# A gated recurrence followed by an MLP on one core: a list scheduler in the kernel sets every engine's order, the activation becomes a linear term plus relu(-h)

## The chip, the cores and the metric

The kernel runs on one core of one Trainium2 chip. The metric is device time in microseconds (us): 1410.16 us before, the median of three runs between 1408.06 and 1410.41. The core's engines are TensorE (PE, matmuls; PEld, its weight loads), VectorE (DVE), ScalarE (ACT) and GpSimd (POOL). SyncE (SP) issues DMA transfers. Each engine works through its own instructions strictly in the order in which the program holds them, and semaphores tie the engines together. So an instruction that waits also holds up all that stands behind it on its engine.

## The reference

Batch 4, 8 heads, sequence 768, head dimension 48, all float32. A complex gate decays a state matrix per head; then an MLP works on the 3072 tokens.

```python
def _attn_ref(q, k, v, a_re, a_im):
    mag = np.sqrt(a_re * a_re + a_im * a_im)
    scale = np.minimum(mag, 0.999) / (mag + 1e-06)
    a_re_n, a_im_n = (a_re * scale, a_im * scale)
    for t in range(S):
        ar, ai = (a_re_n[:, :, t, :, None], a_im_n[:, :, t, :, None])
        new_re = ar * S_re - ai * S_im
        new_im = ar * S_im + ai * S_re
        kv = np.einsum('bhd,bhe->bhde', k[:, :, t], v[:, :, t])
        S_re, S_im = (new_re + kv, new_im)
        y[:, :, t] = np.einsum('bhd,bhde->bhe', q[:, :, t], S_re)
def _moe_ref(x, w_in, w_out, alpha):     # x: 3072 x 384, d_ff 2048
    h = x @ w_in
    g = np.maximum(h, 0.0) + alpha * np.minimum(h, 0.0)
    return g @ w_out
```

## The kernel before

The recurrence is worked in 24 units, one for each batch and each chunk of 128 tokens (`NU = 24`, `NCH = 6` chunks a batch).

- `gates` turns a_re and a_im into decays (`decs`) and rotations (`phs`) for one to three chunks at once. It is a long chain between DVE and ACT: the normalised gate, then running complex products in groups of eight (`product`, three DVE instructions each), then a scan over the groups. Both results go to DRAM.
- `first_halves` copies half rows of v, for five of the level widths, from DRAM to DRAM (`vsc`, L330); `load` brings a unit's q, k, rotations `PP`, decays `T`, and v in several layouts into SBUF. It loads q and k twice (L342/L343 and again L349/L350). All DMAs are issued from SP.
- `unit` multiplies q and k by the rotation (L369), then goes through levels of width 1, 2, 4 ... 64. For each level `meet` makes scores on PE (`ps_lv`, L378), masks them on DVE or ACT (L388, L386, L382), and DVE multiplies halves of q and k by decays (L427). Level 1 has an extra product of the odd rows ("odd"). Then the state is updated (`ps_kt`, `ps_kv`, `St`) and the outputs are summed (`ps_y`, L465, L472), copied to `yT` and written to DRAM as `ysc` (L482).
- `weights` converts w_in and w_out from 64-bit words in 32 pieces (`to_f32`: two ACT, four DVE and two POOL instructions a piece, L297 and L298), in the three `ot` buffers.
- `mlp` takes two units (256 tokens): 16 times three matmuls of w_in with `xT` (L495), relu(-h) on ACT (L499), h + (1 - alpha) relu(-h) on DVE (L501), then 2 x 16 matmuls with w_out (L508).

What sets the order: a loop over slots (`LAG = 6` slots a unit). In each slot the live units go one step on; `gates`, `weights`, `first_halves` and `mlp` are spread over given stretches of slots by `spread`. A fp32 matmul of the program shows as two records in the trace, so that 576 matmuls of L495 are x1152 there; a transpose is one record.

Of the kernel before, what the change touches and what calls it, by code (L numbers as in the profile page):

```python
# [15 lines left out]
P = 128  # L16
# [5 lines left out]
F64_SMALL = 2.0 ** -15 + 2.0 ** -18  # L22


@with_exitstack
def kernel(
# [53 lines left out]
    dram = ctx.enter_context(tc.tile_pool(name="dram", bufs=2, space=DRAM))  # L80
# [11 lines left out]
    def mask(name, h, s):  # L92

        m = work.tile([P, P // h, h * s], F32, tag="neg", name="mask", bufs=2)
# [20 lines left out]

    scr_of = {}
# [9 lines left out]
    def gates(b, c0, c1):  # L126
        C = c1 - c0
        n = C * P
        first, last = c0 == 0, c1 == NCH
        TT = nc.vector.tensor_tensor  # L130
        STT = nc.vector.scalar_tensor_tensor
        ab = work.tile([P, 2, NK * GT], F32, tag="ab", name="ab", bufs=1)[:, :, 0:NK * n]
        tmp = work.tile([P, 4, NK * GT], F32, tag="tmp", name="tmp", bufs=1)[:, :, 0:NK * n]
        dec = decays_sb[:, 0:NK * C]
        for r, src in ((0, a_re), (1, a_im)):
            rows = src[b].rearrange("n i d s -> (n i d) s").rearrange("(t p) s -> p t s", p=P)
            nc.sync.dma_start(ab[:, r].rearrange("p (t s) -> p t s", t=NK), rows[:, :, c0 * P:c1 * P])
        x, y = ab[:, 0], ab[:, 1]
        c, d, e, f = [tmp[:, i] for i in range(4)]

        nc.scalar.activation(c, x, AF.Sign, bias=bias_tiny)
        STT(out=x, in0=c, scalar=TINY, in1=x, op0=ALU.mult, op1=ALU.add)
        nc.scalar.activation(c, x, AF.Square, scale=GATE_SCALE)
        nc.scalar.activation(d, y, AF.Square, scale=GATE_SCALE)
        TT(out=c, in0=c, in1=d, op=ALU.add)
        yield

        nc.scalar.activation(d, c, AF.Abs_reciprocal_sqrt)
        nc.scalar.activation(e, d, AF.Square)
        TT(out=e, in0=e, in1=c, op=ALU.mult)  # L150
        STT(out=d, in0=e, scalar=3.0, in1=d, op0=ALU.subtract, op1=ALU.mult)
        TT(out=c, in0=c, in1=d, op=ALU.mult)
        yield

        nc.scalar.activation(e, d, AF.Identity, scale=-MAG_EPS * GATE_SCALE, bias=bias_two)
        nc.scalar.activation(f, e, AF.Square)
        nc.scalar.activation(f, f, AF.Abs_reciprocal_sqrt)

        for t in (x, y):
            STT(out=t, in0=t, scalar=-0.5 * GATE_SCALE, in1=d, op0=ALU.mult, op1=ALU.mult)  # L160
        yield
        TT(out=e, in0=e, in1=f, op=ALU.mult)
        STT(out=f, in0=e, scalar=2.0, in1=f, op0=ALU.subtract, op1=ALU.mult)

        nc.scalar.activation(c, c, AF.Copy, scale=1.0 / GATE_SCALE)
        STT(out=dec[:, :, 0:P], in0=c.rearrange("p (m s) -> p m s", s=P), scalar=-2.0 * MAG_CAP,
            in1=f.rearrange("p (m s) -> p m s", s=P), op0=ALU.max, op1=ALU.mult)
        yield

        L = 8  # L170
        nb = NK * n // L
        UT = tmp[:, 1:3].rearrange("p r (l n) -> p r l n", l=L)
        nc.scalar.copy(UT[:, 0], x.rearrange("p (n l) -> p l n", l=L))
        nc.scalar.copy(UT[:, 1], y.rearrange("p (n l) -> p l n", l=L))
        at = 0
        while at < TL - 2:
            m = (TL - at) // 2
            pairs = dec[:, :, at:at + m].rearrange("p m (n s) -> p m n s", s=2)
# [3 lines left out]
        phs = dram.tile([2, H * D, n], F32, tag="phs", name="phs")  # L182
        for u in range(b * NCH + c0, b * NCH + c1):
            scr_of[u] = (scr, phs, u - b * NCH - c0)
        nc.sync.dma_start(scr.rearrange("(t p) c s -> p t (c s)", p=P),
                          dec.rearrange("p (t c) s -> p t (c s)", t=NK))
        yield

        def product(dst, j, u, w, m, k):
# [4 lines left out]
            TT(out=dst(0, j), in0=m[:, 0, 0], in1=m[:, 1, 1], op=ALU.subtract)  # L194
            TT(out=dst(1, j), in0=m[:, 0, 1], in1=m[:, 1, 0], op=ALU.add)


        for j in range(1, L):
            product(lambda r, j: UT[:, r, j], j, UT[:, :, j], UT[:, :, j - 1], f, nb)
            if j % 2:  # L200
                yield


        R = 8
        nr = n // L // R
        rows = NK * nr
        blk = work.tile([P, 2, NK * GT // L], F32, tag="blk", name="blk", bufs=1)[:, :, 0:nb].rearrange(
            "p r (l n) -> p r l n", l=R)
        off = work.tile([P, 2, NK * GT // L], F32, tag="off", name="off", bufs=1)[:, :, 0:nb]
        run = work.tile([P, 2, NK, GT // L // R + 1], F32, tag="run", name="run", bufs=1)[:, :, :, 0:nr + 1]  # L210
        runs = work.tile([P, 2, NK * GT // L // R], F32, tag="runs", name="runs", bufs=1)[:, :, 0:rows]
        ends = UT[:, :, L - 1].rearrange("p r (n l) -> p r n l", l=R)
        nc.scalar.copy(blk.rearrange("p r l n -> p r n l"), ends)
        for j in range(1, R):
            product(lambda r, j: blk[:, r, j], j, blk[:, :, j], blk[:, :, j - 1], f, rows)
        yield
# [5 lines left out]
        ends = blk[:, :, R - 1].rearrange("p r (t n) -> p r t n", t=NK)  # L222
        for j in range(nr):
            product(lambda r, j: run[:, r, :, j + 1], j, ends[:, :, :, j], run[:, :, :, j], f, NK)
        if not last:
            nc.vector.tensor_copy(carry, run[:, :, :, nr])
        nc.vector.tensor_copy(runs.rearrange("p r (t n) -> p r t n", t=NK), run[:, :, :, 0:nr])
        yield
        offv = off.rearrange("p r (n l) -> p r l n", l=R)
        nc.vector.tensor_copy(offv[:, :, 0], runs)  # L230
        k = rows * (R - 1)
        ma = f[:, 0:k].rearrange("p (l n) -> p l n", l=R - 1)
        mb = f[:, k:2 * k].rearrange("p (l n) -> p l n", l=R - 1)

        def rb(i):
            return runs[:, i].unsqueeze(1).to_broadcast([P, R - 1, rows])

        for o, (i, op) in enumerate(((0, ALU.subtract), (1, ALU.add))):
            TT(out=ma, in0=blk[:, i, 0:R - 1], in1=rb(0), op=ALU.mult)
            TT(out=mb, in0=blk[:, 1 - i, 0:R - 1], in1=rb(1), op=ALU.mult)  # L240
            TT(out=offv[:, o, 1:R], in0=ma, in1=mb, op=op)

        n2 = f[:, 0:2 * nb].rearrange("p (r n) -> p r n", r=2)
        nc.scalar.activation(n2, off, AF.Square)
        TT(out=n2[:, 0], in0=n2[:, 0], in1=n2[:, 1], op=ALU.add)
        nc.vector.tensor_scalar(out=n2[:, 0], in0=n2[:, 0], scalar1=-0.5, scalar2=1.5, op0=ALU.mult, op1=ALU.add)
        TT(out=off, in0=off, in1=n2[:, 0].unsqueeze(1).to_broadcast([P, 2, nb]), op=ALU.mult)
        yield


        def ob(i):
            return off[:, i].unsqueeze(1).to_broadcast([P, L, nb])

# [348 lines left out]
```

## Time and profile before

| what | value |
|---|---|
| runs before | 1408.06, 1410.16, 1410.41 us |
| the profiled execution | 1410.16 us, of which the span from the first to the last instruction is 1408.3 us |
| instructions | 22177 |
| mean granted TensorE clock | 0.804 |
| ACT busy | 447.3 us (32%) |
| POOL busy | 93.5 us (7%) |
| DMA packets | 240998, 157.96 MB, mean 112 GB/s |

The profiled execution is itself the median of the three runs, so a sum made against its span needs only the 1.9 us around it. Busy is the union of an engine's instructions; a wait is put down to the instruction that ended last before the waiting one began. The granted clock is given as a share of full speed.

### The profile page before, as it was taken

What the parts mean: (1) busy time and instruction counts of PE and PEld (TensorE: products, weight loads), DVE (VectorE), ACT (ScalarE), POOL (GpSimd) and SP (SyncE); (2) the same over time, 40 slices, a digit from 0 to 9 for tenths busy, and PEclk for the clock granted to TensorE, in tenths of its full rate; (3) what the DMA queues carried; (4) which work ended last, traced back from release to release, by engine and by line L of the source; (5) the groups of instructions that cost most, each with busy time, mean ns of one, the idle gap of its engine ahead of it and who ended that gap; (6) DMA issues with size and microseconds to landing.
All of it is one profiled execution on the core that took longest, in us unless ns stands there. A gap on an engine that the chain in (4) does not pass through costs nothing.

```text
span 1408.3 us, 22177 instructions
## 1 busy us (share of the span) xinstructions
PE 910.9 (65%) x8864; PEld 678.6 (48%) x8864; DVE 839.1 (60%) x1703; ACT 447.3 (32%) x845; POOL 93.5 (7%) x96
## 2 busy tenths in 40 slices
PE   0210315052876949917685949927594969998998
PEld 0110214041655638616554638626464747676765
DVE  5287896686444984377434984377533996553511
ACT  3143433432223523152222522152212624231411
POOL 3032141401200000000000000000000000000000
PEclk9999655555876967955896976955796989999999
DMA  3846254812569477096119386185309565775000
GB/s 93 184 117 173 84 116 126 179 48 69 103 125 199 113 146 147 23 202 103 39 35 223 78 180 113 59 168 113 63 9 223 112 157 117 154 134 110 7 29 12
DMA packets 240998, 157.96 MB, mean 112 GB/s; under 512 B 72576, under 2 KB 235776, under 8 KB 240896
## 3 DMA queue, kind: packets, MB, share of 16 engines
q1 hardware_dynamic: 240896, 156.55, 51.4%
q8 instruction: 70, 1.15, 0.4%
q14 instruction: 32, 0.26, 0.1%
HBM read 128.20 MB, written 40.11 MB: 120 GB/s over the span
## 4 chain that ended last, share of the span: by engine, by line
PE 51%; DVE 24%; DMA 9%; ACT 6%; SPq 4%; issue 3%; POOL 1%; POOLq 0%; DVEq 0%; ACTq 0%
PE ps_h L495 19%; PE ps_o L508 15%; PE ps_lv L378 8%; DMA KQ<-in_k_dram 4%; PE ps_y L465 3%; DVE KQ L427 3%; DVE tmp L192 3%; PE ps_kv L442 3%; SPq L330 2%; PE ps_y L472 2%; DVE KQ L369 2%; PE ps_kt L438 2%; DVE top L284 1%; POOL rest L297 1%; ACT yT L481 1%
## 5 line engine op out<-in xcount | busy, mean ns | idle before, releaser
L495 PE MATMUL ps_h<-xT,w_in_sb 128*128 128x256 f32 x1152 | 289.8, 409 | 65.9 <-DVE g L501 35.4
L378 PE MATMUL ps_lv<-KQ 96*64 96x64 f32 (+1 forms) x1152 | 74.7, 295 | 322.2 <-DVE KQ L369 313.7
L495 PEld LDWEIGHTS ps_h<-xT,w_in_sb 128*128 128x128 f32 x1152 | 227.2, 205 | 111.4 <-DVE g L501 35.4
L508 PE MATMUL ps_o<-w_out_sb,g 128*128 128x384 f32 x768 | 266.2, 500 | 6.6 <-POOL w_out_sb L298 4.0
L378 PEld LDWEIGHTS ps_lv<-KQ 96*64 96x64 f32 x1152 | 63.6, 179 | 335.1 <-issue 266.2
L427 DVE TENSOR_TENSOR KQ<-KQ,T 96x512 f32<-96x512 f32 x280 | 187.2, 685 | 46.4 <-PE ps_lv L378 27.8
L508 PEld LDWEIGHTS ps_o<-w_out_sb,g 128*128 128x128 f32 x768 | 145.0, 193 | 105.2 <-issue 6.0
L501 DVE SCALAR_TENSOR_TENSOR g<-neg,rest_al,ps_h 128x256 f32<-128x256 f32 x192 | 90.9, 479 | 156.2 <-ACT neg L499 155.0
L378 PE MATMUL ps_lv<-KQ,W 96*64 96x64 f32 x1920 | 103.4, 262 | 56.3 <-DVE KQ L427 41.2
L499 ACT ACTIVATE neg<-ps_h 128x256 f32<-128x256 f32 x192 | 72.7, 382 | 171.1 <-PE ps_h L495 164.2
L378 PEld LDWEIGHTS ps_lv<-KQ,W 96*64 96x64 f32 x1920 | 87.2, 169 | 80.7 <-issue 46.6
L395 ACT COPY W<-KQ 96x512 f32<-96x512 f32 x120 | 74.9, 624 | 98.1 <-DVE KQ L427 64.9
L369 DVE TENSOR_TENSOR KQ<-KQ,PP 96x2048 f32<-96x2048 f32 x24 | 55.3, 2306 | 79.0 <-DMA Vodd<-in_v_dram 48.9
L465 PE MATMUL ps_y<-A,VL 64*48 64x64 f32 x1920 | 71.2, 257 | 26.6 <-DVE A L388 16.9
L465 PEld LDWEIGHTS ps_y<-A,VL 64*48 64x48 f32 x1920 | 50.9, 143 | 39.5 <-DVE A L388 19.3
L388 DVE TENSOR_TENSOR A<-ps_lv,mask 128x512 f32<-128x512 f32 (+1 forms) x96 | 46.7, 486 | 31.5 <-PE ps_lv L378 30.8
L388 DVE TENSOR_TENSOR Aodd<-ps_lv,maskodd 128x256 f32<-128x256 f32 x24 | 10.1, 422 | 92.6 <-PE ps_lv L378 92.5
L297 POOL TENSOR_TENSOR rest<-rest,top 128x384 f32<-128x384 f32 x32 | 41.9, 1311 | 287.0 <-DVE top L293 244.9
L513 ACT COPY ot<-ps_o 128x384 f32<-128x384 f32 x24 | 11.5, 478 | 149.0 <-PE ps_o L508 149.0
L465 PE MATMUL ps_y<-A,V 64*48 64x128 f32 (+1 forms) x768 | 47.3, 293 | 12.9 <-ACT yT L481 11.0
L261 ACT COPY tmp<-ab 128x1152 f32<-128x1152 f32 (+2 forms) x18 | 35.3, 1960 | 47.0 <-DVE ab L258 45.8
L386 ACT ACTIVATE A<-ps_lv,rows 128x64 f32<-128x64 f32 x144 | 37.3, 332 | 38.4 <-PE ps_lv L378 37.9
(91 smaller groups left out, 1057.7 us busy)
## 6 DMA issues: line engine op xcount, KB each, us to landing
KQ<-in_q_dram SPq DMA_DIRECT2D x96, 192.0 KB
KQ<-in_k_dram SPq DMA_DIRECT2D x96, 192.0 KB
T<-decs SPq DMA_DIRECT2D x48, 384.0 KB
vsc<-in_v_dram SPq DMA_DIRECT2D x80, 144.0 KB
VL<-vsc SPq DMA_DIRECT2D x24, 480.0 KB
PP<-phs SPq DMA_DIRECT2D x48, 192.0 KB
decs<-decays_sb SPq DMA_DIRECT2D x7, 1152.0 KB
phs<-tmp SPq DMA_DIRECT2D x14, 576.0 KB
```

The costliest lines, as they stand in the source:

```text
L192: TT(out=m, in0=u.unsqueeze(2).to_broadcast([P, 2, 2, k]), in1=w.unsqueeze(1).to_broadcast([P, 2, 2, k]), op=ALU.mult)
L297: nc.gpsimd.tensor_tensor(out=rest, in0=rest, in1=top, op=ALU.mult)
L369: nc.vector.tensor_tensor(out=KQ, in0=KQ, in1=PP.unsqueeze(1).to_broadcast([D2, 2, H, P]), op=ALU.mult)
L378: nc.tensor.matmul(t[64 * i:64 * i + 64, p], lhsT=weights(4 * i + p), rhs=moving(KQ[:, 0, 4 * i + p]), start=True, stop=True)
L388: nc.vector.tensor_tensor(out=a, in0=t, in1=masks[name].unsqueeze(1).to_broadcast([P, HP, n]), op=ALU.mult)
L395: nc.scalar.copy(W.rearrange("p n t -> p (n t)").rearrange("p (m h) -> p m h", h=h), halves(KQ[:, 1].rearrange("p n t -> p (n t)"), h)[:, ...
L427: nc.vector.tensor_tensor(out=x, in0=x, in1=decays(h)[:, i].unsqueeze(3).to_broadcast([D2, H, n, h]), op=ALU.mult)
L465: nc.tensor.matmul(o, lhsT=Vp[name][64 * i:64 * i + 64, s, e * D:(e + 1) * D], rhs=A[name][64 * i:64 * i + 64, 2 * s + e], start=(name == ...
L495: nc.tensor.matmul(t, lhsT=w_in_sb[:, kk, f * P:(f + 1) * P], rhs=xT[:, kk], start=(kk == 0), stop=(kk == NK - 1))
L499: nc.scalar.activation(neg, t, AF.Relu, scale=-1.0)
L501: nc.vector.scalar_tensor_tensor(out=gt, in0=neg, scalar=rest_al[:, f:f + 1], in1=t, op0=ALU.mult, op1=ALU.add)
L508: nc.tensor.matmul(t, lhsT=G[f][:, c * P:(c + 1) * P], rhs=w_out_sb[:, f], start=(f == 0), stop=(f == NF - 1))
```

## The change

1. All orders come from a list scheduler that runs while the kernel is built. Each part is a generator; before each instruction (or group of matmuls) it yields the engine, a cost, what it comes after and which ring slots it takes. `Plan.run` always takes the step that can start earliest by those costs, and between steps that start within 0.02 us of each other the one with the earlier due time. `mlp` has the last due time of all. Tile's own scheduling is off (`tc.manual_schedule`).
2. g = h + (1 - alpha) relu(-h) is split. The linear part is x @ (w_in @ w_out): the kernel forms `C_sb` = w_in @ w_out once, from 48 transposes and 48 matmuls, and adds three matmuls with it to each of the 24 sums. (1 - alpha) is multiplied into w_out. L501 goes, and `g` is the relu alone.
3. Level 1: even and odd rows meet their own kind first ("own"), then odd meets even. `Q` is multiplied by decays in halves.
4. `load` is split into `loads` and `loads_v`. q and k are loaded once. All layouts of v come through `vsc` (eight kinds, not five); for batch 0 the 32 copies are issued from POOL.
5. `product` takes two DVE instructions, some small copies of `gates` go to ACT, and the two POOL multiplications of the weights go to DVE. The `mlp` groups are 1, 1, ten of 2, and 1, 1 units.

```diff
+class Plan:
+    HOP = 0.15
+    LAND = 2.0
+    RATE = 170.0
...
+            now = min(t for t, _ in ready) + 0.02
+            t, task = min(((t, k) for t, k in ready if t <= now), key=lambda x: x[1][2])
...
+    def DVE(n, *after, takes=()):
+        return "DVE", 0.17 + n * 1.05e-3, after, takes
+    def DMA(kb, *after, takes=()):
+        return "SP", 0.5, after, takes, kb
...
-            TT(out=m, in0=u.unsqueeze(2).to_broadcast([P, 2, 2, k]),
-               in1=w.unsqueeze(1).to_broadcast([P, 2, 2, k]), op=ALU.mult)
-            TT(out=dst(0, j), in0=m[:, 0, 0], in1=m[:, 1, 1], op=ALU.subtract)
-            TT(out=dst(1, j), in0=m[:, 0, 1], in1=m[:, 1, 0], op=ALU.add)
+            TT(out=m, in0=w[:, 1::-1].unsqueeze(2).to_broadcast([P, 2, 2, k]), in1=pairs_of(u), op=ALU.mult)
+            t = yield DVE(2 * k)
+            TT(out=dst, in0=m[:, 0], in1=m[:, 1], op=ALU.add)
...
-        nc.gpsimd.tensor_tensor(out=rest, in0=rest, in1=top, op=ALU.mult)
-        nc.gpsimd.tensor_tensor(out=dst, in0=num, in1=rest, op=ALU.add)
+        nc.vector.tensor_tensor(out=rest, in0=rest, in1=top, op=ALU.mult)
+        nc.vector.tensor_tensor(out=dst, in0=num, in1=rest, op=ALU.add)
...
+                nc.tensor.transpose(p[:, c], w_in_sb[:, c, f * P:(f + 1) * P], ident)
+                nc.tensor.matmul(sums[c], lhsT=wt[:, c], rhs=w, start=(f == 0), stop=(f == NF - 1))
+            nc.scalar.activation(w, w, AF.Copy, scale=rest_al[:, f:f + 1])
...
+                    (nc.sync if b else nc.gpsimd).dma_start(dst.rearrange("c (m h) e -> m h c e", m=src.shape[0]), src)
...
-        for i in range(2):
-            rows = slice(i * D, (i + 1) * D)
-            nc.sync.dma_start(KQ[rows, 0], qv[b, :, :, cols])
-            nc.sync.dma_start(KQ[rows, 1], kv_in[b, :, :, cols])
...
-        nc.vector.tensor_tensor(out=Q, in0=Q, in1=Tq.unsqueeze(3).to_broadcast([D2, H, HC, 2]), op=ALU.mult)
+        nc.vector.tensor_tensor(out=Q[:, :, :, 0], in0=Q[:, :, :, 0], in1=decays(1)[:, 0], op=ALU.mult)
...
-            neg = work.tile([P, MT], F32, tag="neg", name="neg", bufs=2)
-            nc.scalar.activation(neg, t, AF.Relu, scale=-1.0)
-            gt = work.tile([P, MT], F32, tag="g", name="g", bufs=NF + 1)
-            nc.vector.scalar_tensor_tensor(out=gt, in0=neg, scalar=rest_al[:, f:f + 1], in1=t,
-                                           op0=ALU.mult, op1=ALU.add)
+            nc.scalar.activation(gt, p, AF.Relu, scale=-1.0)
...
+            for kk in range(NK):
+                nc.tensor.matmul(p, lhsT=xT[:, kk, cols], rhs=C_sb[:, kk], start=False, stop=(kk == NK - 1))
...
+        plan.add(loads_x(), -1.0, -1.0, 1)
+        plan.add(all_mlp(), now, now, 1)
```

In the middle of the program, PE's order before had the `mlp` matmuls in long runs and the small matmuls of the units in others:

```order
L465 MATMUL ps_y<-A_2029,VL 48x2x32 x4
L495 MATMUL ps_h<-xT,w_in_sb 128x256 x12
L508 MATMUL ps_o<-w_out_sb,g 128x384
L495 MATMUL ps_h<-xT,w_in_sb 128x256 x36
L508 MATMUL ps_o<-w_out_sb,g 128x384 x31
L378 MATMUL ps_lv<-KQ 64x64 x16
L378 MATMUL ps_lv<-KQ 64x128 x8
```

Here 48 and 32 matmuls of one `mlp` stand together, between the units' levels. PE after, around its row 430 of 942:

```order
L815 MATMUL ps_o<-w_out_sb,g 128x384 x10
L606 MATMUL ps_lv<-KQ,W 64x64 x8
L820 MATMUL ps_o<-C_sb,xT 128x384 x3
L606 MATMUL ps_lv<-KQ,W 64x64 x8
L799 MATMUL ps_h<-xT,w_in_sb 128x256 x3
L606 MATMUL ps_lv<-KQ,W 64x64 x8
L799 MATMUL ps_h<-xT,w_in_sb 128x256 x3
L606 MATMUL ps_lv<-KQ,W 64x64 x8
L799 MATMUL ps_h<-xT,w_in_sb 128x256 x5
```

A level of a unit (L606, eight matmuls) now stands between a few matmuls of `mlp`. At the very end, behind the last unit's `ps_y`, PE holds nothing but `mlp` (rows 925 to 940 of 942):

```order
L799 MATMUL ps_h<-xT,w_in_sb 128x256 x43
L815 MATMUL ps_o<-w_out_sb,g 128x384 x16
L820 MATMUL ps_o<-C_sb,xT 128x384 x3
L815 MATMUL ps_o<-w_out_sb,g 128x384 x16
L820 MATMUL ps_o<-C_sb,xT 128x384 x3
L799 MATMUL ps_h<-xT,w_in_sb 128x256 x48
```

SP's order at the start, before: all copies for batch 0, then the first unit.

```order
L330 DMA vsc<-in_v_dram 64x6x96 x20
L185 DMA decs<-decays_sb 128x3x256
L262 DMA phs<-tmp 128x3x128 x2
L342 DMA KQ<-in_q_dram 48x8x128
L343 DMA KQ<-in_k_dram 48x8x128
L344 DMA PP<-phs 48x8x128
```

These 20 copies are no longer on SP. SP after, rows 26 to 31 of 344; `VL` waits for all 32 copies that POOL issues, and `PP` and `T` of the first unit stand behind it:

```order
L430 DMA raw<-in_w_in_dram 128x3x256
L579 DMA VL<-vsc 128x8x192
L430 DMA raw<-in_w_out_dram 128x768
L561 DMA PP<-phs 48x8x128 x2
L568 DMA T<-decs 48x8x256 x2
L550 DMA KQ<-in_q_dram 48x8x128
```

The copies themselves now stand at the end of POOL's queue, behind the masks:

```order
L535 DMA vsc<-in_v_dram 64x6x96
L172 COPY mask_119<-mask 64x64 x2
L535 DMA vsc<-in_v_dram 64x6x96 x31
```

More of the change, by code (lines that the diff above doesn't have):

```diff
@@ L217, in gates @@
+        t = yield from three(blk3.rearrange("p r l n -> p r n l"),
+                             UT[:, :, L - 1].rearrange("p r (n l) -> p r n l", l=Rn), t)
+        for j in range(1, Rn):
+            t = yield from product(blk[:, :, j], blk3[:, :, j], blk[:, :, j - 1], f, rows, t)
+        t = yield from three(ends, blk[:, :, Rn - 1], t)
+        t = yield DVE(10, t)
         if first:
@@ L228, in gates @@
[L228 to L241, printed above, removed]
+        t = yield from three(runs.rearrange("p r (t n) -> p r t n", t=NK), run[:, :, :, 0:nr], t)
@@ new lines, in mlp, with all_mlp @@
+            t = yield ACT(DM, e, takes=(R["ot"],))
+            ot = work.tile([P, DM], F32, tag="ot", name="ot", bufs=3)
+            nc.scalar.copy(ot, p)
+            R["o"].put(t)
+            t = yield DMA(197, t)
+            nc.sync.dma_start(out[row + c * P:row + (c + 1) * P], ot)
+            R["ot"].put(t)
+        R["xT"].put(e)
+    def all_mlp():
+        for m in range(len(sizes)):
+            yield from mlp(m)
+    for name in ("own", 2, 4, 8):
+        mask(name, 1 if name == "own" else name, 1)
```

718 lines of the change are left out of this document (482 added, 236 removed).

## The prediction

> **What bounds the kernel now.** I read the page first, then the waits, then busy time by stretch, then the order of time on PE.
>
> ```profile
> span 1408.3 us, 22177 instructions
> PE 910.9 (65%) x8864; PEld 678.6 (48%) x8864; DVE 839.1 (60%) x1703; ACT 447.3 (32%) x845; POOL 93.5 (7%) x96
> ...
> PE   0210315052876949917685949927594969998998
> ...
> DVE  5287896686444984377434984377533996553511
> ...
> PE 51%; DVE 24%; DMA 9%; ACT 6%; SPq 4%; issue 3%; POOL 1%; POOLq 0%; DVEq 0%; ACTq 0%
> ```
>
> No engine is near full. In the slices, PE and DVE take turns: where one shows 9 the other shows 3 to 5. The chain that ended last is PE for half and DVE for a quarter. So the time is an alternation, not one engine's load. The waits say the same:
>
> ```profile
> PE ps_lv L378 <- DVE KQ L369: 313.7, 12, 58.3
> POOL rest L297 <- DVE top L293: 244.9, 28, 65.6
> DVE g L501 <- ACT neg L499: 155.0, 137, 22.7
> ...
> SPq L482 <- ACT yT L481: 299.8, 40, 30.9
> ```
>
> PE stood 12 times, 314 us together, until the next unit's rotation (L369), with no MLP matmul in its queue. SP's queue, in order, stood 300 us at the `ysc` stores with later loads behind them.
>
> ```profile
> 770.00:840.00 70.00, 56.24 (x625) 39.82 (x623) 63.00 (x140) 30.53 (x56) 0.00 (x0) 0.90 0.59 122
> ...
> 1120.00:1190.00 70.00, 58.97 (x648) 43.54 (x647) 57.32 (x136) 23.39 (x48) 0.00 (x0) 0.88 0.58 126
> 1190.00:1260.00 70.00, 67.78 (x761) 50.41 (x760) 40.51 (x64) 21.17 (x54) 0.00 (x0) 1.00 0.71 145
> 1260.00:1330.00 70.00, 66.36 (x746) 49.52 (x746) 34.61 (x59) 21.09 (x54) 0.00 (x0) 0.95 0.38 79
> ```
>
> Columns: length, PE, PEld, DVE, ACT, POOL busy, granted clock, DMA share, GB/s. PE's busy share times its clock is what PE does of its full speed: 0.72 and 0.74 in the first two, where the gates load DVE to 0.90 and 0.82; 0.97 and 0.90 in the last two, where units and MLP run without gates.
>
> **What PE has to do at full clock.** From dense rows:
>
> ```profile
> 1187.15 0.69 PE L378 MATMUL ps_lv<-KQ,W 96*64 96x64 f32 x16
> 1187.77 2.86 PE L495 MATMUL ps_h<-xT,w_in_sb 128*128 128x256 f32 x12
> ...
> 1200.41 1.57 PE L378 MATMUL ps_lv<-KQ 96*64 96x64 f32 x32
> 1207.17 0.49 PE L438 MATMUL ps_kt<-ident,KQ 96*128 96x96 f32 x4
> ...
> 1215.45 0.44 PE L465 MATMUL ps_y<-A,V 64*48 64x128 f32 x8
> ...
> 1218.80 0.64 PE L378 MATMUL ps_lv<-KQ,W 96*64 96x64 f32 x16
> ```
> ```profile
> 1156.16 2.29 DVE KQ L369
> ...
> 1210.13 1.45 PE ps_kv L442 x16
> ...
> 1362.38 20.99 PE ps_h L495 x96
> 1383.37 10.33 PE ps_o L508 x32
> 1394.26 10.60 PE ps_o L508 x32
> ```
>
> One record costs 20.99/96 = 0.219 us in `ps_h` and 10.33/32 = 0.323 in `ps_o`. A level takes 0.62 us (start to start, 1187.15 to 1187.77), 32 records from strided KQ 1.5, a unit's `ps_y` 3.35 (1215.45 to 1218.80), `kt` 8 x 0.12 = 1.0, `kv` 1.5.
> Before: `ps_h` 1152 x 0.219 = 252; `ps_o` 768 x 0.323 = 248; levels 24 x 5.5 = 132 (odd 0.75, level 1 about 1.05, six of 0.62); `ps_y` 80, `kt` and `kv` 20 units x 2.5 = 50. Sum 762 us, of a span of 1408.
> After: `ps_h` the same 252 (the 128-column groups at half the cost each, an assumption; bounded above by no saving, 21 us more). `ps_o` gains 72 matmuls, 144 records: 912 x 0.323 = 295. C costs 48 matmuls x 2 x 0.323 = 31 and 48 transposes x 0.12 = 6. Levels: "own" has 32 records, 1.5, and seven levels of 0.62, so 24 x 5.84 = 140. `ps_y`, `kt`, `kv` 130. Sum 854: PE gets 92 us more work, and all the gain must come from waits.
>
> **DVE, ACT, DMA.**
>
> ```profile
> L427 DVE TENSOR_TENSOR KQ<-KQ,T 96x512 f32<-96x512 f32 x280 | 187.2, 685 | 46.4 <-PE ps_lv L378 27.8 <-ACT W L395 18.0
> L501 DVE SCALAR_TENSOR_TENSOR g<-neg,rest_al,ps_h 128x256 f32<-128x256 f32 x192 | 90.9, 479 | 156.2 <-ACT neg L499 155.0
> ...
> L415 DVE TENSOR_TENSOR KQ<-KQ,T 96x1024 f32<-96x1024 f32 x24 | 29.1, 1211 | 0.0
> ...
> L284 DVE SCALAR_TENSOR_TENSOR top<-top,raw 128x384 f32<-128x384 f32 x32 | 24.1, 752 | 35.9 <-ACT top L283 35.9
> ...
> L283 ACT ACTIVATE top<-raw 128x384 f32<-128x384 f32 x32 | 17.5, 548 | 67.3 <-POOL rest L297 60.1 <-DMA raw<-in_w_out_dram 7.2
> L194 DVE TENSOR_TENSOR tmp<-tmp 128x144 f32<-128x144 f32 x49 | 14.8, 302 | 0.6
> L195 DVE TENSOR_TENSOR tmp<-tmp 128x144 f32<-128x144 f32 x49 | 14.6, 299 | 0.0
> ...
> L288 DVE TENSOR_SCALAR num<-top 128x384 uint32<-128x384 uint32 x32 | 11.4, 355 | 1.6
> ...
> L448 DVE TENSOR_TENSOR St<-St,T 96x384 f32<-96x384 f32 x16 | 8.8, 551 | 18.6 <-PE ps_y L472 12.7 <-ACT St L446 5.9
> ...
> L247 DVE TENSOR_TENSOR off<-off,tmp 128x288 f32<-128x288 f32 x7 | 3.2, 456 | 0.2
> ```
>
> DVE loses L501, 90.9. Level 1 replaces a 1.211 us by a 0.685: 24 x 0.53 = 13. `product` replaces 302 + 299 ns by one 288-element add (456 ns): 0.145 each; with the small ones 174 products, about 25. Merged and moved copies in the gates save some 9 (estimate from their counts). L284 at 752 ns, against 551 for 384 elements in L448, shows what POOL's work beside it cost: 32 x 0.2 = 6. DVE gains 64 multiplications and additions for the weights at 0.551: 35. Net 839 - 91 - 13 - 25 - 9 - 6 + 35 = 730. ACT gains a third strided copy in the gates, 16 scalings and 16 copies for C, some small copies: about 45, so 490 of 1050, hidden beside PE and DVE. If ACT's order delays a relu, PE waits; `ps_h` has two buffers for that.
>
> ```profile
> q1 hardware_dynamic: 240896, 156.55, 51.4%
> ...
> KQ<-in_q_dram SPq DMA_DIRECT2D x96, 192.0 KB
> ```
>
> Of q and k every second load goes (96 of these, 18.9 MB); v's relayout adds 14 MB by three more kinds and saves 7 MB of small loads. About 145 MB are left: at 51.4% x 1408 / 156.55 = 4.6 us a MB some 670 us of DMA time, 63% of the new span. It stays under PE.
>
> **The sum by stages.** PE is now the largest load (854, DVE 730), and PE's order keeps MLP matmuls between the levels, so it can work while DVE rotates. But MLP needs `xT` of unit 0 and all weights, so there is a start.
>
> Start, up to unit 1's first matmul. The 32 pieces pass through three `ot` buffers, so one at a time: ACT 0.548, then DVE 0.55 + 0.355 + 0.55 + 0.355 + 0.55 + 0.55 = 2.91, together 3.46, or 111 us. The first starts at about 20 (the first gate's load and chain come first). DVE does unit 0 (15) and the gates of two chunks (730 - 366 units - 93 weights = 271, over 24 chunks 11.3 each: 25 with the start of the next) in between. Low: no wait at all, 20 + 93 + 15 + 25 = 153. High: nothing overlaps, 171, and 8 for the copies below, 179. I take 165.
>
> The copies for batch 0 stand on POOL, and unit 0's PP and T stand behind VL on SP, which waits for all 32. No row shows a DMA issued from POOL. The nearest:
>
> ```profile
> 1.82 29.74 SPq L330 DMA_DIRECT2D vsc<-in_v_dram  x20
> ```
> ```profile
> 27.56 4.00 SPq L330
> ...
> 56.00 2.28 DVE KQ L369
> ```
>
> The same copies from SP took 29.74/20 = 1.49 us each, the slowest 4.0. At 1.49 they end at 14 + 48 = 62, unit 0 rotates at about 70 (56 before), and DVE has 58 us of other work ahead of it: little is lost. At 4.0 they end at 142, and 80 us are lost, since the remaining pieces stand behind the rotation on DVE. I take 1.49, because it is the same transfer in the same early stretch. Better than 1.49 gains nothing more than the 8.
>
> ```profile
> 79.15 1.48 DVE L427 TENSOR_TENSOR KQ<-KQ,T 96x512 f32<-96x512 f32 x1
> ```
>
> POOL and DVE do hold each other up here: this L427 took 1.48 instead of 0.685 beside a POOL multiplication. [...]
>
> Middle, from there to the last `ps_y`. PE has left 854 less C and unit 0 (37 + 12) less the end (below, 134): 671 us at full clock. The share of full speed lies between 0.73 (gates beside it) and 0.94 (the mean of the last two stretches). DVE's load in this stage is about 590 of 750, 0.79, near the first two stretches, which speaks for the low end. But there DVE also had to make `g` for the MLP (L501), which no longer exists, and PE had nothing else queued while it waited. I take 0.89: 671/0.89 = 754. That also covers the gates' chain, which must run seven times for three chunks each: 34 us of DVE and some 21 of ACT plus waits, below the 103 us that three units take.
>
> End, behind the last `ps_y`: 91 matmuls of 256 columns x 0.437 + 96 of half that + 114 x 0.646 = 40 + 21 + 74 = 135 (134 taken), dense as in the last rows above, and 4 for the store. Sum 165 + 754 + 134 + 4 = 1057, and 1.9 around the span (1410.16 - 1408.3; that execution is the median): 1059 us.
>
> **Rivals.**
> PE keeps waiting: an order fixed at build time from fixed costs runs late somewhere, and PE stays at 0.74 as beside the gates before. Then 671/0.74 = 907, and 1212 in all. For it: DVE's 0.79, and clocks of 0.88 to 0.90 in those stretches. Against it: no DVE step in the MLP, MLP spread between levels.
> POOL's copies are late, 4.0 us each: 1059 + 80 = 1139. For it: L427's 1.48 beside POOL; against it: 1.49 from SP. [...]
> Near the bound: PE at 0.98 and the start at 155 give 155 + 685 + 138 + 2 = 980.
> Slower than before: SP's queue. If each unit's loads stand behind the store of the one before, units run one after the other. From its rotation at 1156.16 to the end of its `ps_y` at 1218.80 a unit took 63 us; 22 x 63 + 303 = 1689. It decides from 50 us a unit ((1410 - 305)/22). Against it: KQ has three buffers, and SP's order has later loads ahead of the stores.
>
> **How the numbers follow.** Forecast (PE share 0.83 to 0.96, start as taken: 1000 to 1115) 0.55; PE keeps waiting 0.16; POOL late 0.13; near the bound 0.13; slower than before 0.03. The predicted time is 1059. The range goes from 975 (near the bound, PE at 0.98 and the start at its low) to 1155 (POOL late, or PE at 0.79); it leaves out most of the PE rival, 0.10, the slower one, 0.03, and some 0.04 below. A difference within 0.2% would be no change by this measurement: 0.01. Faster 0.96, slower 0.03.
>
> **What would show it.** PE busy over 85% of the span with a clock above 0.9 from about 165 us on; the wait of `ps_lv` for the rotation gone from 314 to below 50; DVE near 730; about 135 us at the end with only MLP on PE; the first rotation at about 70 us. Wrong if the first rotation comes after 100 us, if the granted clock in the middle is below 0.85, or if PE waits for DVE's level steps.

## The result, and the profile after

| kernel | median us | runs | ratio to before, 95% interval |
|---|---|---|---|
| before | 1410.29 | 1408.06 to 1414.02 (4) | |
| after | 1188.26 | 1182.89 to 1197.59 (4) | 0.843, 0.8366 to 0.8495 |

The change takes 222 us away, and 129 us less than predicted: 1188 is outside the range of 975 to 1155. The profiled run took 1183.68 us, its span 1182.0. Everything below is set against the predicted span of 1057, so 125 us are to be found.

From the page of after: span, busy time, slices of 29.6 us (PE, DVE, granted clock) and the chain that ended last by engine.

```profile
span 1182.0 us, 24063 instructions
PE 964.3 (82%) x10112; PEld 692.0 (59%) x10112; DVE 747.4 (63%) x1347; ACT 489.8 (41%) x984; POOL 37.4 (3%) x59
...
PE   0425646687858899998898899989898989999998
...
DVE  6768787874977488767665885878387737500000
...
PEclk9865676887957999998999999989998989999999
...
PE 74%; DVE 10%; ACT 9%; issue 4%; DMA 2%; SPq 1%; DVEq 0%; ACTq 0%
```

PE is now the bound: 74% of the chain where it had 51%, and 8 or 9 in every slice from the 13th on. Ahead of that, up to about 380 us, it is not: PE shows 8 at most, mostly at a clock of 5 to 8. The stretches say how much (columns as in the prediction: length, PE, PEld, DVE, ACT, POOL busy, granted clock, DMA share, GB/s).

```profile
0.00:199.00 199.00, 84.00 (x447) 48.39 (x447) 153.66 (x347) 86.52 (x164) 37.41 (x59) 0.73 0.61 155
199.00:380.00 181.00, 132.99 (x1651) 105.89 (x1651) 137.83 (x240) 79.91 (x158) 0.00 (x0) 0.75 0.58 130
380.00:1041.00 661.00, 611.15 (x7406) 438.06 (x7404) 455.91 (x761) 298.47 (x591) 0.00 (x0) 0.96 0.60 136
1041.00:1182.00 141.00, 136.18 (x626) 99.67 (x615) 0.00 (x0) 24.89 (x73) 0.00 (x0) 0.99 0.04 13
```

PE's busy share times its clock is 0.55 from 199 to 380 us, 0.89 from 380 to 1041 us, and 0.96 in the end, where only the MLP is left. In the slow stretch PE is idle for 48 of the 181 us, and busy at a clock of 0.75. Unit 1's first matmul comes at 199.0, not at 165. The waits that answer to the ones of before (in all, times, longest):

```profile
ACT w_out_sb L507 <- PE ps_c L504: 56.9, 16, 6.5
...
PE ps_lv L606 <- ACT W L674: 42.6, 17, 5.2
PE ps_c L504 <- DVE w_out_sb L469: 41.9, 11, 6.9
...
PE ps_lv L606 <- DVE KQ L668: 12.3, 7, 7.2
```

The wait of `ps_lv` for a rotation, 313.7 us before, is down to 1.4 us. New is the first row: ACT stands 16 times, once in each pair of weight pieces, at the scaling of w_out.

### The profile page after: what moved, and what is told of

Its sections match the earlier page's. It is cut to its first block, busy times and chain, and to the rows that moved or that the text cites. A ratio compares the mean times of both kernels' runs of the same rounds, so it can differ in the third digit from the quotient of the medians.

```text
span 1182.0 us, 24063 instructions
## 1 busy us (share of the span) xinstructions
PE 964.3 (82%) x10112; PEld 692.0 (59%) x10112; DVE 747.4 (63%) x1347; ACT 489.8 (41%) x984; POOL 37.4 (3%) x59
## 2 busy tenths in 40 slices
DMA packets 201941, 146.36 MB, mean 124 GB/s; under 512 B 58984, under 2 KB 195664, under 8 KB 201832
## 4 chain that ended last, share of the span: by engine, by line
PE 74%; DVE 10%; ACT 9%; issue 4%; DMA 2%; SPq 1%; DVEq 0%; ACTq 0%
PE ps_o L815 22%; PE ps_h L799 22%; PE ps_lv L606 9%; PE ps_y L748 5%; PE ps_o L820 4%; PE ps_c L504 4%; ACT tmp L283 3%; PE ps_lv L649 3%; PE ps_kv L711 3%; PE ps_y L756 2%; DMA KQ<-in_q_dram 1%; PE ps_kt L701 1%; DVE KQ L668 1%; ACT tmp L398 1%; ACT W L674 1%
## 5 line engine op out<-in xcount | busy, mean ns | idle before, releaser
L799 PE MATMUL ps_h<-xT,w_in_sb 128*128 128x256 f32 (+1 forms) x1344 | 297.2, 373 | 6.5 <-ACT g L805 6.4
L668 DVE TENSOR_TENSOR KQ<-KQ,T 96x512 f32<-96x512 f32 x280 | 190.0, 685 | 143.4 <-PE ps_lv L606 107.9
L805 ACT ACTIVATE g<-ps_h 128x256 f32<-128x256 f32 (+1 forms) x224 | 78.2, 353 | 158.7 <-PE ps_h L799 158.2
L606 PE MATMUL ps_lv<-KQ,W 96*64 96x64 f32 x1920 | 91.8, 244 | 59.6 <-ACT W L674 42.6
L606 PEld LDWEIGHTS ps_lv<-KQ,W 96*64 96x64 f32 x1920 | 74.6, 152 | 103.3 <-ACT W L674 58.8
L504 PE MATMUL ps_c<-w_out_sb,wt 128*128 128x384 f32 x96 | 62.6, 821 | 63.4 <-DVE w_out_sb L469 41.9
L674 ACT COPY W<-KQ 96x512 f32<-96x512 f32 x120 | 74.2, 624 | 25.2 <-DVE KQ L668 16.1
L504 PEld LDWEIGHTS ps_c<-w_out_sb,wt 128*128 128x128 f32 x96 | 28.3, 313 | 86.7 <-ACT top L446 42.2
L769 ACT COPY yT<-ps_y 48x256 f32<-48x256 f32 x96 | 30.9, 366 | 112.7 <-PE ps_y L756 105.0
L283 ACT ACTIVATE tmp<-ab 128x1152 f32<-128x1152 f32 (+2 forms) x27 | 54.9, 2075 | 14.9 <-DVE decays_sb L278 14.9
L748 PE MATMUL ps_y<-A,VL 64*48 64x64 f32 x2688 | 50.9, 225 | 9.6 <-issue 9.6
L596 DVE TENSOR_TENSOR KQ<-KQ,PP 96x2048 f32<-96x2048 f32 x24 | 54.7, 2281 | 0.1
L820 PE MATMUL ps_o<-C_sb,xT 128*128 128x384 f32 x144 | 52.8, 496 | 0.0
L606 PEld LDWEIGHTS ps_lv<-KQ 96*64 96x64 f32 x768 | 30.6, 155 | 32.0 <-issue 14.7
L606 PE MATMUL ps_lv<-KQ 96*64 96x64 f32 x768 | 37.6, 247 | 12.2 <-DVE Aown L629 6.3
```

The lines of the kernel that those rows point to most:

```text
L283: nc.scalar.activation(U3[:, o], p.rearrange("p (n l) -> p l n", l=L), AF.Copy, scale=w)
L504: nc.tensor.matmul(sums[c], lhsT=wt[:, c], rhs=w, start=(f == 0), stop=(f == NF - 1))
L596: nc.vector.tensor_tensor(out=KQ, in0=KQ, in1=PP.unsqueeze(1).to_broadcast([D2, 2, H, P]), op=ALU.mult)
L606: nc.tensor.matmul(t[64 * i:64 * i + 64, p], lhsT=weights(4 * i + p), rhs=moving(KQ[:, 0, 4 * i + p]), start=True, stop=True)
L668: nc.vector.tensor_tensor(out=x, in0=x, in1=decays(h)[:, i].unsqueeze(3).to_broadcast([D2, H, n, h]), op=ALU.mult)
L674: nc.scalar.copy(W.rearrange("p n t -> p (n t)").rearrange("p (m h) -> p m h", h=h), halves(KQ[:, 1].rearrange("p n t -> p (n t)"), h)[:, ...
```

## The experiments

All kernels are the changed kernel with the edit shown, each timed beside the kernel before, whose median was 1408.6 to 1410.3 in every comparison. A time set against 1188 is told apart from it where the intervals of the two ratios to before do not meet.

### The start: what holds the weights' pieces up

PE's rows for the first four products `ps_c` of after (start, duration, six records each, idle time ahead and what ended it):

```profile
38.55 4.18 PE L504 MATMUL ps_c<-w_out_sb,wt 128*128 128x384 f32 x6 [6.90 <-DVE w_out_sb L469]
47.20 3.87 PE L504 MATMUL ps_c<-w_out_sb,wt 128*128 128x384 f32 x6 [3.82 <-DVE w_out_sb L469]
55.52 4.18 PE L504 MATMUL ps_c<-w_out_sb,wt 128*128 128x384 f32 x6 [4.13 <-DVE w_out_sb L469]
64.16 3.87 PE L504 MATMUL ps_c<-w_out_sb,wt 128*128 128x384 f32 x6 [3.82 <-DVE w_out_sb L469]
```

A pair of pieces takes about 8.5 us here, not the 6.92 (2 x 3.46) of the prediction. It is a loop: PE waits for DVE's piece, and its product then takes about 4 us (the third here took 4.18 at a granted clock of 0.50; the one at 134.65 us took 2.20 at 1.00); ACT's scaling (L507) waits for PE; the next piece's first ACT step stands behind it in order; DVE waits for that step.

Experiment `e1_defer` issues the scaling one pair later:

```diff
             R["W"].put(e)
-            t = yield ACT(DM, e)
-            nc.scalar.activation(w, w, AF.Copy, scale=rest_al[:, f:f + 1])
-            done["w_out", f] = t
+            used.append(e)
+            for i in [f - 1] * (f > 0) + [f] * (f == NF - 1):
+                done["w_out", i] = yield ACT(DM, used[i])
+                nc.scalar.activation(w_out_sb[:, i], w_out_sb[:, i], AF.Copy, scale=rest_al[:, i:i + 1])
```

> The changed kernel with one step moved: the scaling of w_out (ACT L507), which waits for the product ps_c of the same piece, is issued one pair of weight pieces later, so that ACT no longer stands at it; the same work otherwise. Theory 1 (the start is a closed loop: ps_c at half clock takes about 4 us, ACT waits for it at L507, the next piece's first ACT step stands behind, DVE idles about 2 us in a pair): a pair falls from 8.6 us to 7.0 to 7.5, 16 of them give 18 to 26 us, unit 1's rotation comes at 171 to 180 us instead of 196.7, and the time falls by half of that to all of it, from 1188 to 1162 to 1179. Rival (the start is set by DVE's own work or by the DMAs, the idle time is a consequence): the rotation stays within 5 us of 196.7 and the time within 3 us of 1188.

Measured: 1171.77 us (ratio 0.8306, 0.8282 to 0.8329). The wait fell from 56.9 to 3.4 us, and unit 1's rotation (L596 in after, L597 here) from 196.67 to 182.17:

```profile
ACT w_out_sb L509 <- PE ps_c L504: 3.4, 1, 3.4
```
```profile
182.17 2.28 DVE L597 TENSOR_TENSOR KQ<-KQ,PP 96x2048 f32<-96x2048 f32 x1
```

So 14.5 us of the late start are ACT's stand, and they all reach the end (16.5 us by the medians). The rotation is 2 us later than the theory's latest: the loop is only part of the late start. The first four pairs take 6.5 us each (8.5 in after), but those between 140 and 172 us 7.9, above the 7.0 to 7.5 expected. What is left shows in the stretch that ends with the rotation:

```profile
20.00:182.17 162.17, 79.74 (x446) 46.74 (x447) 142.84 (x315) 76.56 (x146) 18.97 (x18) 0.70 0.64 157
```

DVE's work is the same, 142.84 us, and it still idles for 19.3.

Experiment `e8_pe_filled` leaves the loop and makes PE busy, with the order of all else as it was (and four such matmuls ahead of each level's product of units 0 to 5):

```diff
+            for _ in range(8):
+                nc.tensor.matmul(p[:, 0], lhsT=ident, rhs=ident, start=True, stop=True)
             for c in range(NK):
                 nc.tensor.transpose(p[:, c], w_in_sb[:, c, f * P:(f + 1) * P], ident)
```

> The changed kernel, in the same order on every engine, with matmuls of no use added on PE: 8 of 128 columns ahead of the transposes of each weight piece (16 times) and 4 of 128 columns ahead of each of the levels' products of units 0 to 5; their results are overwritten. Theory 5 (the low granted clock of the start and of 211 to 380 us, 0.66 and 0.76, follows from PE's gaps, and the slow ps_c of 4 us and the slow levels are what the others wait for): the clock rises above 0.8 in both stretches, ps_c takes about 2.2 us, and the time falls by 10 to 30 us. Rival (the gaps come from DVE's and ACT's order and the clock costs little): the clock rises, the time stays within 8 us of 1188 or rises by up to 20 us, as the added matmuls stand ahead of the useful ones.

Measured: 1172.25 us (0.8324, 0.8303 to 0.8345): 296 matmuls of no use (592 records) made the kernel 16 us faster. PE's rows:

```profile
47.40 2.17 PE L506 MATMUL ps_c<-w_out_sb,wt 128*128 128x384 f32 x6 [2.36 <-DVE w_out_sb L469]
49.41 1.95 PE L495 MATMUL ps_wt<-ident 128*128 128x128 f32 x16
51.20 0.49 PE L497 MATMUL ps_wt<-ident,w_in_sb 128*128 128x128 f32 x3
54.06 2.17 PE L506 MATMUL ps_c<-w_out_sb,wt 128*128 128x384 f32 x6 [2.37 <-DVE w_out_sb L469]
```

In these rows the gaps are 2.4 us, not 3.8 and more, `ps_c` takes 2.17 us, and the pair 6.66. The clock rose from 0.66 to 0.87 between 39 and 211 us. In after's first pairs `ps_c` took 3.9 to 4.2 us behind gaps of 3.8 and more, here 2.17 behind gaps of 2.4. The gap just ahead does not tell it alone, though: in after a `ps_c` takes 4.18 us at 120.16 us, behind a gap of 2.57, and again at 202.20 us, behind 1.47, both at a granted clock of 0.50. What else sets the granted clock was not shown. Unit 1's rotation comes at 183.05, 13.6 us sooner, so most of the gain is again the start. Two edits, one that takes the slow product out of ACT's way and one that makes it fast, give the same 16 us. No run has both.

### 199 to 380 us: PE is fed late

One run of the gates is left out, early (chunks 3 to 5 of batch 0) or late (the same chunks of batch 2); its units take the decays and the rotation of the three units ahead of them. `SKIP` is (0, 3) or (2, 3).

```diff
...
+        if key == SKIP:
+            u0 = key[0] * NCH + key[1]
+            for u in range(u0, u0 + 3):
+                scr_of[u] = scr_of[u - 3]
+                done["T", u], done["PP", u] = done["T", u - 3], done["PP", u - 3]
...
+            if g[:2] == SKIP:
+                continue
             plan.add(gates(*g), *due["gates", g], 100)
```

> The changed kernel without one run of the gates, the early one: chunks 3 to 5 of batch 0 are not worked out, and units 3 to 5 take the rotation and the decays of units 0 to 2. About 60 us of DVE work, 30 us of ACT work and 5 MB of DMA are left out between 190 and 275 us. Theory 2 (until about 380 us PE is short of units, because a run of the gates gives only 3 units in some 105 us and no MLP work is left over): the share of PE's full-clock work in 211 to 380 us rises from 0.59 to 0.75 or more, and the time falls by 30 to 45 us, to 1143 to 1158. Rival (PE is the bound of the middle from the start, as the prediction took it): the time falls by 0 to 8 us.

> The same cut at another place: the gates of chunks 3 to 5 of batch 2 are not worked out, and units 15 to 17 take what units 12 to 14 took; the same amount of work of every engine is left out, in the stretch where PE's full-clock share is 0.88. Theory 2: 0 to 12 us are gained, 1176 to 1188, a third or less of what the early cut gives. Rival (DVE and ACT hold PE up by the same amount everywhere, through waits in order): as much as the early cut, 30 us or more.

Measured: early out 1143.62 us (0.8115, 0.8089 to 0.8141), late out 1180.25 us (0.8365, 0.8339 to 0.8392; its interval meets that of after). The same work is worth 45 us in one place and 8 us or nothing in the other. Busy time in 199 to 380 us, early out first, then late out:

```profile
199.00:380.00 181.00, 148.14 (x2045) 115.49 (x2045) 118.94 (x198) 77.10 (x173) 0.00 (x0) 0.89 0.68 141
```
```profile
199.00:380.00 181.00, 130.26 (x1634) 103.53 (x1635) 136.15 (x239) 78.74 (x155) 0.00 (x0) 0.75 0.57 127
```

PE's share of full speed goes from 0.55 to 0.73 in the first and stays at 0.54 in the second. (The expectation's 0.59 for 211 to 380 us was a count of records; by busy time and clock it is 0.56, and 0.74 in the early one, just below the 0.75 expected.) What PE stood at, in the same stretch, are the level products. Their group in after, then in early out (busy, mean, idle time ahead of it and what ended it):

```profile
L606 PE MATMUL ps_lv<-KQ,W 96*64 96x64 f32 x320 | 18.5, 278 | 30.3 <-ACT W L674 19.1 <-DVE KQ L668 7.2 <-DVE run L352 3.0
```
```profile
L615 PE MATMUL ps_lv<-KQ,W 96*64 96x64 f32 x400 | 18.8, 242 | 4.2 <-ACT W L683 4.2
```

So after 380 us DVE's gates lie beside PE's work and cost next to nothing, and before it they decide when PE gets units. Until then PE waits at the levels of the few units that it has, because there is no stock of MLP work yet: an `mlp` group needs its units complete, and the first three runs of the gates give 1, 2 and 3 chunks. In the 181 us PE runs 222 records of `ps_h` in after (192 of them 128 columns wide), and 288 in early out.

### What the split activation is worth

Experiment `e4_split_undone` puts the activation back and leaves the scheduler as it is:

```diff
-            nc.scalar.activation(gt, p, AF.Relu, scale=-1.0)
+            nc.scalar.activation(neg, p, AF.Relu, scale=-1.0)
+            r = yield DVE(n, r, takes=() if f % 3 else (R["g"],))
+            nc.vector.scalar_tensor_tensor(out=gt, in0=neg, scalar=rest_al[:, f:f + 1], in1=p,
+                                           op0=ALU.mult, op1=ALU.add)
...
-            for kk in range(NK):
-                nc.tensor.matmul(p, lhsT=xT[:, kk, cols], rhs=C_sb[:, kk], start=False, stop=(kk == NK - 1))
```

> The changed kernel with the activation put back alone: ACT makes relu(-h), DVE adds h to its product with 1-alpha; no scaling of w_out, no transposes and no products for C at the start, no C in the output. PE loses 62 us of busy time at the start (ps_c) and 72 matmuls of 0.65 us in the output, 46 us; DVE gains 224 steps of about 0.42 us, 90 us, and each stands in a chain h -> ACT -> DVE -> output with two buffers for h. Theory 3 (the middle is PE's): 30 to 70 us faster than the changed kernel, 1118 to 1158. Rival (the DVE step of lowest rank in the middle of the MLP's chain makes PE wait for DVE's queue, and the MLP piles up behind the attention): 50 to 200 us slower, 1240 to 1390.

Measured: 1395.5 us (0.9896, 0.9869 to 0.9923), 207 us slower than after, although PE has less to do. Theory 3 is out, and the loss is a little over the rival's 200. Its page (PE and DVE by slices of 34.8 us) and one stretch:

```profile
PE   0023066645655675655665693789999999999998
...
DVE  6988978668868878858878859776112211122211
```
```profile
380.00:1041.00 661.00, 451.36 (x6513) 359.32 (x6511) 469.51 (x805) 267.34 (x509) 0.00 (x0) 0.70 0.58 127
```

PE reaches 0.48 of full speed between 380 and 1041 us (451.36/661 x 0.70). DVE is through with the attention at about 975 us (28 slices), and then PE works off the MLP alone for some 420 us. DVE itself is 71% busy in that stretch, so it is not full. The MLP waits because its DVE step has the last due time, behind every attention and gate step. To tell the step from its rank, the rank alone was changed, with the split undone (`e5_split_undone_ranked`) and with the split kept (`e10_ranked`):

```diff
-        plan.add(all_mlp(), now, now, 1)
+        plan.add(all_mlp(), 150.0, now + 50.0, 1400)
```

> The kernel with the split activation undone (1395.5 us), with one more line changed: the MLP's task gets a rank that rises from 150 us to the end, among the attention's, in place of the last rank of all, so that DVE's step in its chain is put ahead of gate and attention steps that come due later. Theory 4 (the loss of 207 us is one of rank: the planner puts a DVE step of the last rank behind all attention work, the MLP piles up until DVE is done near 1000 us, and PE idles meanwhile): most of it comes back, 1170 to 1250 us. Rival (the DVE step costs by itself, through its place in the chain h -> ACT -> DVE -> output or DVE's 98 us): still over 1320 us.

> The changed kernel, split activation and all, with the rank of the MLP's task alone changed as in the kernel with the split undone and ranked (1163.7 us): rising from 150 us to the end in place of last of all. Theory 4 (it is the order that decides, and the split only makes the last rank bearable, since it takes DVE out of the MLP's chain): the rank gives the split nothing, PE's MLP work now stands ahead of attention work that DVE waits for, and the time is 1188 to 1235 us. Rival (the rank is worth 25 us or more in both, and the split is worth something besides): 1130 to 1165 us.

Measured: undone and ranked 1163.73 us (0.8264, 0.8252 to 0.8276), 6 us below what was expected, kept and ranked 1213.6 us (0.863, 0.8592 to 0.8668). One line takes 232 us off the kernel with the old activation, which is then 25 us faster than after, and puts 25 us on the kernel with the split. There DVE waits longer for level matmuls ("DVE KQ L668 <- PE ps_lv L606" is 136.8 us, 107.9 in after), as it would with MLP matmuls ahead of them; that these make up the 25 us was not shown. So the split as such does not make the gain. It makes the last rank bearable, by taking DVE out of the MLP.

### The copies of v on POOL

`e6_v_on_sp` issues them from SP again:

```diff
-                        end = yield "POOL", 1.0, (), (), 147
+                        end = yield DMA(147)
-                (nc.sync if b else nc.gpsimd).dma_start(dst.rearrange("c (m h) e -> m h c e", m=src.shape[0]), src)
+                nc.sync.dma_start(dst.rearrange("c (m h) e -> m h c e", m=src.shape[0]), src)
```

> The changed kernel with the 28 copies of v of batch 0 issued by SP again and not by POOL; nothing else. The trace shows them gone from POOL by 39.4 us, about 1.0 us each. Theory (SP has room in the start, the copies were no load on either queue): 1188 within 10 us. Rival 1 (on SP they stand ahead of the first gates' loads or of the weights' pieces, 28 copies of about 0.5 to 1 us): 15 to 30 us slower. Rival 2 (the copies' DMAs slowed the start wherever they are issued): no change in the first rotation, 88 us, within 5 us.

Measured: 1186.9 us (0.8424, 0.8411 to 0.8436), no difference. (There are 32 copies; the 28 of the expectation was a miscount.) The first rotation is at 90.3 us, 88.6 in after, as rival 2 has it too. What made the first rotation late is in DVE's own stretch ahead of it in after:

```profile
14.00:88.64 74.64, 20.32 (x41) 10.41 (x42) 56.83 (x135) 32.83 (x58) 24.52 (x26) 0.79 0.79 191
```

DVE had 56.83 us of work there and idled for 17.8, and it came to the rotation without a wait (0.1 us ahead of all 24). Of the idle time, 6.2 us wait for a piece's ACT step and 5.5 for the first ACT step of the next gates, and ACT stands at the scaling (L507) for 17.5 us there; neither waits for a DMA. In `e1_defer`, with the copies as they were, the first rotation is at 79.8. With the copies on SP ACT does wait for a DMA, a piece of w_out, once and 6.7 us. POOL's rows in after:

```profile
10.68 4.53 POOL L535 DMA_DIRECT2D vsc<-in_v_dram  x7
...
16.73 22.66 POOL L535 DMA_DIRECT2D vsc<-in_v_dram  x23 [0.50 <-DMA vsc<-in_v_dram]
```

### Putting it together

`e9_reordered` keeps the split for all but the last two `mlp` groups, which go without C, and changes the order and the stand at L507. The whole diff is longer; these are some of its lines, and `rest_al` holds alpha - 1 here:

```diff
-    RATE = 170.0
+    RATE = 200
...
-        for o, (p, w) in enumerate(((y, -1.0), (x, 1.0), (y, 1.0))):
-            tu = yield ACT(2 * N, tx, t)
+        for o, p, w, need in ((1, x, 1.0, tx), (2, y, 1.0, tz), (0, y, -1.0, t)):
+            tu = yield ACT(2 * N, tx, need)
...
-            nc.scalar.activation(w, w, AF.Copy, scale=rest_al[:, f:f + 1])
...
-            nc.scalar.activation(gt, p, AF.Relu, scale=-1.0)
+            nc.scalar.activation(gt, p, AF.Relu, scale=rest_al[:, f:f + 1])
...
-    GATES = [(0, 0, 1), (0, 1, 3), (0, 3, 6)] + [(b, c, c + 3) for b in range(1, B) for c in (0, 3)]
+    GATES = [(0, 0, 2), (0, 2, 4), (0, 4, 6)] + [(b, c, c + 2) for b in range(1, B) for c in (0, 2, 4)]
```

> The changed kernel with what the runs so far point to, no work left out: gates in groups of two chunks, so that a run of the gates ends sooner; w_out not scaled, 1-alpha is ACT's scale at relu; the three strided copies of a run of the gates in the order in which their inputs come; the planner's DMA rate 200 GB/s in place of 170, weights due 30 us sooner and the next gates due a little sooner; the last two groups of the MLP without C, with h added on DVE, which is idle by then. Theory 1 and 2 together (PE is fed late; its own work is some 850 us): PE's full-clock share rises in 211 to 380 us to 0.7 or more, and the time comes to 1095 to 1140. Rival (order is worth little, what holds is PE's and DMA's own pace): 1165 or more.

Measured: 1091.38 us (0.7737, 0.7712 to 0.7761), 97 us faster than after. Unit 1 rotates at 132.72 (the first run of the gates now gives two chunks), and PE does 0.85 of full speed from 199 to 380 us:

```profile
199.00:380.00 181.00, 162.53 (x2104) 122.65 (x2100) 141.28 (x269) 97.38 (x203) 0.00 (x0) 0.95 0.66 148
```

What each of its changes gives was not timed one by one.

`e11_undone_reordered` is the ranked kernel with the split undone, with an order of its own (from its diff against that with the split undone):

```diff
-            e = yield PE(0.45 * n / HC, *after, takes=(R["lv"],))
+            e = yield PE(0.65 * n / HC, *after, takes=(R["lv"],))
...
-    GATES = [(0, 0, 1), (0, 1, 3), (0, 3, 6)] + [(b, c, c + 3) for b in range(1, B) for c in (0, 3)]
+    GATES = [(0, 0, 3), (0, 3, 6)] + [(b, c, c + 3) for b in range(1, B) for c in (0, 3)]
...
-            due["gates", z] = now, now + 0.7 * us
+            due["gates", z] = now, now + 0.3 * us
```

> The split undone, and the order changed for it: the MLP ranked from 150 us to the end, gates in groups of three chunks from the first on, the next gates due sooner, the three strided copies in the order of their inputs, the levels' products at 0.65 and 1.5 us and the output parts at 0.84 us in the planner as the trace has them, weights due 30 us sooner. PE has 777 us of full-clock work in place of 854, DVE 838 us. Theory (with the right order the split is a loss, as it puts 77 us on the engine that is the bound): 1075 to 1120 us, within 20 us of the reordered kernel with the split (1091). Rival (DVE, at 838 us and 76% or more, becomes the bound and its waits for PE come on top): 1130 us or more.

Measured: 1074.17 us (0.7632, 0.7608 to 0.7656), a little below what was expected, the fastest of all, 114 us below after, and without the split. From its page:

```profile
PE 835.1 (78%) x9728; PEld 616.2 (57%) x9728; DVE 815.1 (76%) x1497; ACT 467.6 (44%) x910; POOL 37.6 (3%) x59
...
PE 67%; DVE 16%; issue 4%; ACT 2%; DMA 1%; SPq 0%; DVEq 0%; ACTq 0%
```

PE and DVE are nearly level in busy time, but the chain that ended last is PE's for 67% and DVE's for 16%. As the two kernels have different orders, their 17 us are not the split's alone. The matmuls of no use were then added to both, as in `e8_pe_filled` (in the second only ahead of the levels):

> The reordered kernel with the split (1091.4 us), with the matmuls of no use ahead of the weight pieces' transposes and of the levels' products of units 0 to 5; its order is the same. Theory 5 (a busy PE is granted the full clock, and the start's loops run faster): 1075 to 1085 us. Rival (the reordered kernel's clock of 0.95 in 211 to 380 us leaves nothing to gain, and at the start DVE is the bound): within 5 us of 1091, or slower by up to 10.

> The kernel with the split undone and its own order, with the matmuls of no use ahead of the levels' products of units 0 to 5 alone (there are no transposes of the weights). Theory 5: 5 to 15 us faster than the same kernel without them. Rival (attention alone leaves PE idle for longer than the added matmuls can fill, and the clock stays): no change within 4 us.

Measured: 1102.45 us (0.7831, 0.7809 to 0.7853), 11 slower, and 1080.24 us (0.7669, 0.765 to 0.7689), 6 slower by the medians, but with intervals that overlap. The clock did rise (0.74 to 0.84 between 39 and 211 us in the first, 0.87 to 0.92 between 211 and 380 us in the second), and theory 5 missed twice. In the first, unit 1 rotates at 134.4 (132.7 without them): no ACT scaling stands behind `ps_c` there, and PE is busy for 49 us more. So a higher clock gave time (16 us, `e8`) only in the kernel where ACT stood at the slow product.

## Why the prediction was wrong, point by point

| term of the sum | predicted us | measured us |
|---|---|---|
| start, to unit 1's first matmul | 165 (153 to 179) | 199 |
| middle | 754 | 842 |
| end and store | 138 | 141 |
| span | 1057 | 1182 |

- **The start failed by 34 us**, outside its own bounds, in the term for waits (12 us) and in the one for the gates. DVE's work from the first piece to unit 1's rotation, in the stretch that ends with it:

```profile
20.00:196.67 176.67, 83.08 (x446) 48.39 (x447) 141.85 (x316) 74.57 (x145) 19.39 (x18) 0.69 0.58 144
```

  Of the 141.85 us busy, the weights have 92.5 and unit 0 14.2, summed over DVE's rows (93 and 15 were priced); the gates have the rest, about 35, where "25 with the start of the next" was taken. And DVE idles for 34.8 us, where 165 left 12 for waits. So 10 us go to the gates' term and 23 to the waits. "together 3.46" took ACT and DVE of a piece as the only chain and put the scalings down as "hidden beside PE and DVE", where the scaling behind a `ps_c` of some 4 us was a third party: 14.5 us, by `e1_defer`. The idle time left there, 19.3 us, is still 7 above the 12 taken, and was not taken apart.
- **The middle failed by 88 us, in "I take 0.89".** From 380 us on that is the measured value, 0.89. From 199 to 380 us it was 0.55: 99.7 us of full-clock work in 181 us, where 0.89 would have taken 112, so 69 us went there. The rest is 15 us more work than the 671 (686 by busy time and clock), some 17 us. The step that failed is that PE "can work while DVE rotates" from unit 1 on. It needs MLP groups in stock, and there is none until the gates have run ahead. `e2` against `e3` shows that PE is fed late in that stretch and not after it, and in `e9`, which changes more than that, the share there is 0.85. The signs that were to show the forecast wrong hardly came: the first rotation was ahead of 100 us, the clock from 199 to 1041 us was 0.91, and PE's wait for DVE's level steps was 12.3 us in all. They stood for the whole middle or for the time ahead of it, and the loss sat in its first 181 us.
- **The rival "PE keeps waiting"** gave 1212 by 0.74 for the whole middle, and came nearer than the forecast; that the order was to blame fits `e9`, that its fixed costs were was not tested. But there is not one share: the mean, 686/842 = 0.81, is made of 0.55 and then 0.89.
- **Right:** DVE 747.4 (730 predicted), ACT 489.8 (490), DMA 146.36 MB (145), the wait for rotations, and the end, with its own reason: the matmuls of 128 columns were taken at half the cost of those of 256, and they took 10.99/96 = 0.114 us a record there, where half of 0.219 is 0.11:

```profile
1131.98 10.99 PE L799 MATMUL ps_h<-xT,w_in_sb 128*128 128x128 f32 x96
```

  The bound given with that assumption, 21 us without any saving, should have been 42: there are 384 such records.
- **The first rotation** came at 88.6 us and not at 70. The engine that issued the copies was not the cause: on POOL or SP it is 88.6 or 90.3. DVE had the work ahead of it that was priced (56.8 us, 58 taken), and the 17.8 us for which it idled were not in the sum.
- **The copies on POOL** took 22.66/23 = 0.99 us each, less than the 1.49 taken. DVE was busy for 25.2 of 28.7 us beside them (10.68 to 39.39). The rival of 1139 had them at 4.0 us each, which did not come.
- **The split** was priced by loads, +84 us on PE (47 in `ps_o`, 37 to form C) against -91 on DVE, and taken as what frees PE. The runs show that its worth hangs on the rank of the MLP: 207 us with the last rank, less than nothing with the rising one (1163.7 without the split, 1213.6 with it). That the fastest kernel, 1074.2, is one without it points the same way, but its order is its own.

## What to carry to other kernels

Price the stage in which the stock of work is still being built by itself: there the engine that feeds can be the bound, even if another is the bound of the whole (here PE did 0.55 of its full speed from 199 to 380 us, 0.89 after it, and 0.73 in the first stretch with one run of DVE's gates left out). With engines that work in order, look at each step of the early loop for what it waits for and for what stands behind it; a step that nobody needs yet (here a scaling) belongs one round later. And before work is moved from one engine to another to unblock it, try the rank of the work in the scheduler: one line took 232 us off the kernel with the old activation here, and put 25 us on the one with the split.

## What was not expected of the hardware

Matmuls of no use made a kernel 16 us faster: in its second to fourth pair, with gaps of 2.4 us and not 3.8 or more, six records of `ps_c` took 2.17 us and not 3.9 to 4.2. In a kernel where no scaling waited for `ps_c`, they cost 11 us. And POOL issued DMAs at 0.99 us each while DVE was busy for 25.2 of 28.7 us.
